# A state-space scan with an ELU layer behind it: the last scan products of one pair joined behind three units, 21 wider idle products for 30, and g's low words between y's two word sums

## The chip, the cores and the metric

The kernel runs on 1 core of one Trainium2 chip. The metric is the device time in microseconds (us). The engines are TensorE (PE; its weight loads are listed as PEld), VectorE (DVE), ScalarE (ACT), GpSimd (POOL) and SyncE (SP), which issues nearly all DMAs.

## The reference

For 4 batches x 8 heads x 768 positions, a chunked scan, then a two-layer network on the 3072 tokens:

```python
for c in range(nc):                                  # chunks of the sequence
    L = np.exp(cum[:, :, :, None] - cum[:, :, None, :]) * causal
    M = np.einsum('bhin,bhjn->bhij', Cc, Bc) * L
    y_intra = np.einsum('bhij,bhjd->bhid', M, xc)
    y_inter = np.einsum('bhin,bhnd->bhid', Cc, state) * decay_to_i[:, :, :, None]
    y[:, :, sl] = y_intra + y_inter
    state = decay_full[:, :, None, None] * state + np.sum(Bx, axis=2)
x = y.transpose(0, 2, 1, 3).reshape(B * S, H * D)    # 3072 x 256
h = x @ w_in                                         # 256 -> 2048
g = np.where(h > 0.0, h, np.exp(np.minimum(h, 0.0)) - 1.0)
out = g @ w_out                                      # 2048 -> 256
```

Inputs and output are fp32.

## The kernel before

The tokens are cut into 12 blocks of 256 (`n` = 0 to 11), worked on in pairs. The order of all instructions on each engine is written out by hand; the program runs without loops on the chip.

**Products in words.** From the pair n = 2 on, an fp32 product is made of three passes over operands that have been split into rounded words: a high word, a low word and a sum word. For y, `high_of_y` (L798, ACT) makes y1, `low_of_y` (L806, DVE) makes y0, and `both_of_y` (L816, DVE) makes the sum word y_both, one instruction for each of the two halves k of the 256 input features. For g, a *job* is a generator of three steps (`words_of_g`): ACT's high word (L922), DVE's low word (L923, tile g_low) and POOL's sum word (`sub`, L899, tile g_words). `first_of_jobs`, `second_of_jobs` and `third_of_jobs` issue these steps for jobs begun one or two rounds before.

**A stage.** For n = 4, 6, 8 the loop over `k` = 0 to 15 does three things side by side. `l1_words(n, k, m)` makes 128 rows of h for pair n (TensorE L832: passes high, low and sum; at k = 0 the sum pass is last, at other k it is first), followed on ACT and DVE by L840, L848, L860, L861 and, one round later, L867, which writes g. `l2s(count)` makes so many *units* of the second layer for the pair before (`second(n - 2)`); a unit is six products (L981), which read a job's words. `stage_scan` and the lines around it make the scan of the pair after, `m = n + 2`: `scores`, `weigh`, `sums`, `states`, and last `across` (L660, products with the state, 64 records in the trace) and `inside` (L678, products with x, 128 records). `inside` also copies the finished y to yT, half t = 0 (heads 0 to 3) with ACT (L695), half t = 1 with DVE (L693) for these stages. Both can be called for a half.

**Order around the edited places.** At `k == 13` the last scan products are issued around `l2s(3)`: for n = 4 and n = 8 all of them behind the three units, for n = 6 half t = 0 ahead of the units and half t = 1 behind them. At `k == 14` SP issues a 64-byte load (`held`, L1394) that reads yT and so waits for ACT's copies; the loads of the next stage's weight words (L765, L766) are behind it in SP's queue. At k = 14, `high_of_y` and `low_of_y` of the next pair are made, and no second or third steps of jobs. At `k == 15` (`m == MC - 1` in `l1_words`) DVE makes both halves of y_both, then g_low of one job, and POOL that job's L899; the first unit of the next stage reads it right after the first `l1_words`, whose third pass reads y_both. POOL also makes the decays of later pairs, `decay_sums` (L536), after `k == 12`.

**Start.** `small_idle_products(30, 112)` gives TensorE work on a tile of zeros while the first loads are under way: each call of matmul works on 32 rows x 64 columns of the array, at one of eight positions in turn, and is two records in the trace. The first real products are `first_low` (L501) and `first_cum` (L512, L520).

Of the kernel before, what the change touches and what calls it, by code (L numbers as in the profile page):

```python
# [13 lines left out]
F32R = mybir.dt.float32r  # L14
# [3 lines left out]
P = 128  # L18
Q = 64
BLK = 2 * P  # L20
# [13 lines left out]
def kernel(  # L34
# [36 lines left out]
    KC, MC = DM // P, DF // P  # L71
# [4 lines left out]
    ffn = ctx.enter_context(tc.tile_pool(name="ffn", bufs=2))  # L76
# [191 lines left out]
    def small_idle_products(count, cols):  # L268

        banks = [ps_idle] + [psum([P, 4, P], "ps_idle") for _ in range(3)]  # L270
        for k in range(count):
            rows, at = slice(32 * (k % 4), 32 * (k % 4) + 32), Q * (k // 4 % 2)
            nc.tensor.matmul(
                out=banks[k % 4][at:at + Q, 0:2, 0:cols], lhsT=idle[rows, 0:Q],
                rhs=idle[rows, 0:cols].unsqueeze(1).to_broadcast([32, 2, cols]),
                start=True, stop=True, tile_position=(32 * (k % 4), at), skip_group_check=True)

    small_idle_products(30, 112)
    ident = const.tile([P, P], F32, name="ident")
    make_identity(nc, ident)  # L280

# [105 lines left out]
    yT = {}  # L387
# [257 lines left out]
    def across(*ns, pool=p_a, tag="a", halves=(0, 1)):  # L645


        y = [None, None]
        for t in halves:
            y[t] = [psum([P, len(ns), 2, Q], "ps_y"), (p_a if t else pool).tile(  # L650
                [P, len(ns), 2, Q], F32, tag="a" if t else tag, name="ps_y")]
        for u in (1, 0):
            for at, n in enumerate(ns):
                for v in range(2):
                    Sx = starts.get((n, u, v))
                    if Sx is None:
                        continue
                    for q in range(2 * halves[0], 2 * halves[-1] + 2):
                        rows, col = slice(32 * q, 32 * q + 32), (64 * q + shift(n, v)) % P
                        nc.tensor.matmul(  # L660
                            out=y[q // 2][v][col:col + 64, at, u],
                            lhsT=Sx[rows].rearrange("p k d -> p (k d)"),
                            rhs=st[n]["cts"][rows, u, Q * v:Q * v + Q],
                            start=(u == 1 and at == 0), stop=False,
                            tile_position=(32 * q, col), skip_group_check=True)
        return y
# [120 lines left out]
    y_words = {}  # L787
# [20 lines left out]
                op0=ALU.mult, op1=ALU.subtract)  # L808
        y_words[n] = y1, y0

    def both_of_y(n):
        y = yT[n // 2].rearrange("p k b u i -> p k (b u i)")
        y1, y0 = y_words[n]
        both = ffn.tile([P, KC, 2 * BLK], F32R, tag="yT", name="y_both")
        for k in range(KC):
            nc.vector.scalar_tensor_tensor(  # L816
                out=both[:, k], in0=y1[:, k].bitcast(F32), scalar=1.0 - WORD,
                in1=y[:, k], op0=ALU.mult, op1=ALU.add)
        y_words[n] = y1, y0, both

    def l1_words(n, m, ahead=None, ahead_of_join=(), ahead_of_jobs=()):


        cols = slice(m % 2 * P, (m % 2 + 1) * P)
        w, w0 = k_words[m // 2]
        w1, both_w, w0 = w[:, 0, :, cols], w[:, 1, :, cols], w0[:, :, cols]
        y1, y0, both_y = y_words[n]
        high, both = psum([P, 2 * BLK], "ps_h"), psum([P, 2 * BLK], "ps_w")
        passes = [(high, w1, y1), (high, w0, y0), (both, both_w, both_y)]
        for ps, lhs, rhs in passes if n > 2 and m == 0 else passes[2:] + passes[:2]:  # L830
            for k in range(KC):
                nc.tensor.matmul(  # L832
                    out=ps, lhsT=lhs[:, k], rhs=rhs[:, k], start=k == 0 and lhs is not w0,
                    stop=k == KC - 1 and lhs is not w1)
        if ahead and m == MC - 1:
            both_of_y(ahead)
            second_of_jobs()
            third_of_jobs()
        e = ffn.tile([P, 2 * BLK], F32, tag="e", name="e", bufs=2)
        nc.scalar.activation(e, both, ACT.Copy, scale=WORD)  # L840
        first_of_jobs()
        if late:
            end_words()
        if ahead and m == MC - 2 and n > 2:
            high_of_y(ahead)
        for step in ahead_of_join:
            step()
        nc.vector.scalar_tensor_tensor(  # L848
            out=high, in0=high, scalar=WORD - 1.0, in1=e, op0=ALU.mult, op1=ALU.add)
        if ahead and m == MC - 2 and n > 2:  # L850
            low_of_y(ahead)
        for step in ahead_of_jobs:
            step()
        if not ahead or m != MC - 2:
            second_of_jobs()
        late.append((n, m, high, e))
# [106 lines left out]
    def second_of_jobs():  # L963

        while put_second:
            put_second.pop(0)()
        if len(begun_jobs) > 1:
            for j in begun_jobs[0]:
                next(j)

    def third_of_jobs():

        if len(begun_jobs) > 1:
            for j in begun_jobs.pop(0):
                next(j)
# [384 lines left out]
    for n in range(4, NP, 2):  # L1360
        m = n + 2 if n + 2 < NP else None
        steps = second(n - 2)

        def l2s(count):
            for _ in range(count):
                next(steps)

        if n == 4:
            l2s(1)
        if not m:  # L1370
            scan_pools.close()
            late_pool = ctx.enter_context(tc.tile_pool(name="late", bufs=1))
        for k in range(16):
            if k < 13 and (n > 4 or k > 4):
                to_begin.append(lambda q=k + 3: job(n - 2, q))
            elif m and k > 12:
                to_begin.append(lambda q=k - 13: job(n, q))
            if not m and k in (4, 6, 8, 10, 12, 14, 15):
                to_begin.append(lambda q=(4, 6, 8, 10, 12, 14, 15).index(k): late_job(q, late_pool))
            if k == 0 and n > 4:  # L1380
                load_words(2)
            l1_words(
                n, k, m, [lambda q=q: weigh_two(m, q) for q in (2, 3) if m and k == 10],
                [lambda: states(m + 1)] if m and k == 11 else [])
            if k != 14 or not m:
                third_of_jobs()
            if n == 4 and k < 2:
                words_of_w(k + 2)
            if n == 4 and 1 < k < 7:
                words_of_out(k + 1)  # L1390
            if k in (2, 4, 6, 8, 10) and (k > 2 or n > 4):
                load_words(k // 2 + 2)
            if m and k == 14:
                nc.sync.dma_start(out=held, in_=yT[m // 2][Q:Q + 1, 0, 0, 0, Q:Q + 16])  # L1394
            if m and k > 13:
                load_words(k - 14)
            if m:
                stage_scan(n, k)
            begin_end()
            if n == 4 and k in (1, 2):  # L1400
                low_of_w(k + 1)
                keep_words(k + 1)
            if n == 4 and 2 < k < 8:
                low_of_out(k)
            if not m:
                l2s(2)
                continue
            if k == 9:
                l2s(1)
                scores(m, m + 1, pool=p_o, tag="o")  # L1410
            l2s((2 - (n == 4 and k < 1), 2, 2, 2, 2, 2, 2, 2, 2, 1, 2, 2, 1, 0, 1, 0)[k])
            if k == 9:
                for q in range(2):
                    weigh_two(m, q)
            if k == 10:
                if m + 2 < NP:
                    for to in (m + 2, m + 3):
                        spread_cum(to)
                sums(m, m + 1, pool=p_o, tag="o")
                states(m)  # L1420
            if k == 13:
                if n == 6:
                    y = across(m, m + 1, pool=p_o, tag="o", halves=(0,))
                    inside(y, m, m + 1, t=0)
                l2s(3)
                if n == 6:
                    y = across(m, m + 1, halves=(1,))
                    inside(y, m, m + 1, t=1)
                else:
                    y = across(m, m + 1, pool=p_o, tag="o")  # L1430
                    inside(y, m, m + 1)
            if k == 12 and m + 2 < NP:
                decay_sums(m + 2)
                decay_sums(m + 3)
        if m:
            l2s(3)
        end_words()
        for _ in steps:
            pass
# [46 lines left out]
```

## Time and profile before

| | |
|---|---|
| median of 3 runs | 339.98 us (339.45 to 340.72) |
| profiled execution | 338.85 us |
| its span, first to last instruction | 337.1 us |
| mean granted TensorE clock | 0.999 |
| busy: PE, DVE, ACT, POOL | 98%, 85%, 77%, 64% of the span |
| HBM read, written | 44.53 MB, 9.63 MB |

The profile is of one execution; its times are microseconds from the first instruction. A busy TensorE is not one at its peak, since matmuls overlap. In the lists of waits, the engine and line ahead of the arrow waited for those behind it; "issue" is time in which the engine waited for nothing that the profile shows. In the timeline, the time in brackets is idle time of the engine just before, and what ended it.

### The profile page before, as it was taken

Reading aid. Unit: us, or ns where it says so; the run is one execution under the profiler, and the core shown is the slowest. Engines: PE = TensorE matmul, PEld = TensorE weight load, DVE = VectorE, ACT = ScalarE, POOL = GpSimd, SP = SyncE. Lnnn points to the kernel's source line nnn. Section 1 sums busy time; section 2 is a strip of 40 time slices with the busy share of each in tenths; the row PEclk is TensorE's granted clock in tenths of the full one; section 3 lists DMA queues with packets and bytes.
Section 4 is the critical chain, followed back from the end, with each engine's and each line's share of the span. In section 5 each row is a group of like instructions: output and inputs, shape, how many; then the busy total and the mean of one; then the engine's idle time right before and its main releaser. Section 6 shows DMA issues by size and latency. Waiting matters only on the chain.

```text
span 337.1 us, 9647 instructions
## 1 busy us (share of the span) xinstructions
PE 330.4 (98%) x3742; PEld 288.2 (85%) x3742; DVE 286.7 (85%) x511; ACT 259.0 (77%) x537; POOL 214.2 (64%) x242
## 2 busy tenths in 40 slices
PE   8899999999999999999999999999999999999995
PEld 5578888888888888888899988889889899999995
DVE  4998998889897889898989998989996978997942
ACT  5789989599857699857898866898867789897501
POOL 5454554648979396989489979388974355776000
PEclk9999999999999999999999999999999999999999
DMA  8889999553487388671769491669440762330101
GB/s 141 218 237 181 293 193 277 127 108 123 158 158 290 126 217 272 200 185 16 272 189 215 138 300 27 263 188 191 126 156 8 277 212 101 104 118 0 33 0 63
DMA packets 82956, 54.79 MB, mean 163 GB/s; under 512 B 59038, under 2 KB 68574, under 8 KB 82910
## 3 DMA queue, kind: packets, MB, share of 16 engines
q1 hardware_dynamic: 80734, 53.98, 57.4%
q8 instruction: 29, 0.48, 0.6%
q10 hardware_dynamic: 2176, 0.20, 0.5%
q14 instruction: 17, 0.14, 0.1%
HBM read 44.53 MB, written 9.63 MB: 161 GB/s over the span
## 4 chain that ended last, share of the span: by engine, by line
PE 92%; SPq 2%; DMA 2%; ACT 2%; DVE 1%; issue 0%; DVEq 0%; ACTq 0%
PE ps_o L981 24%; PE ps_h L832 20%; PE ps_o L885 12%; PE ps_h L717 11%; PE ps_w L832 10%; PE ps_both L981 6%; PE ps_y L678 3%; DMA w<-in_moe_w_in_dram 2%; PE ps_g L582 2%; PE ps_y L660 2%; PE ps_st L612 1%; PE ps_high L981 1%; SPq L156 1%; SPq L184 0%; ACT w_in L214 0%; SPq L124 0%
## 5 line engine op out<-in xcount | busy, mean ns | idle before, releaser
L899 POOL TENSOR_TENSOR g_words<-g_words,g_low 128x512 fp32r<-128x512 f32 x62 | 82.3, 1331 | 49.2 <-DVE g_low L923 25.8
L981 PE MATMUL ps_o<-o_words,g_words 128*128 128x256 f32 x448 | 83.4, 284 | 0.0
L981 PEld LDWEIGHTS ps_o<-o_words,g_words 128*128 128x128 f32 x448 | 72.9, 190 | 5.8 <-POOL g_words L899 0.8
L860 ACT ACTIVATE e<-ps_h 128x512 f32<-128x512 f32 x72 | 43.0, 597 | 35.1 <-DVE ps_h L848 35.1
L867 DVE SCALAR_TENSOR_TENSOR g<-e,ps_h 128x512 f32<-128x512 f32 x72 | 49.3, 684 | 19.0 <-ACT e L861 17.1
L981 PE MATMUL ps_o<-o_low,g_low 128*128 128x256 f32 x224 | 63.3, 283 | 0.0
L923 DVE SCALAR_TENSOR_TENSOR g_low<-g_words,g 128x512 fp32r<-128x512 f32 x72 | 63.3, 885 | 0.0
L848 DVE SCALAR_TENSOR_TENSOR ps_h<-ps_h,e 128x512 f32<-128x512 f32 x72 | 49.8, 691 | 2.7 <-ACT e L840 2.6
L832 PE MATMUL ps_w<-y_both,w_words 128*128 128x512 f32 x144 | 48.7, 419 | 0.0
L861 ACT ACTIVATE e<-e 128x512 f32<-128x512 f32 x72 | 45.5, 633 | 2.3
L717 PE MATMUL ps_h<-yT,w_in 128*128 128x256 f32 (+1 forms) x208 | 45.2, 367 | 1.6 <-ACT yT L695 1.0
L840 ACT ACTIVATE e<-ps_w 128x512 f32<-128x512 f32 x72 | 41.9, 582 | 5.4 <-PE ps_w L832 5.4
L885 PE MATMUL ps_o<-w_out,g 128*128 128x256 f32 x192 | 45.5, 380 | 0.0
L832 PE MATMUL ps_h<-y,w_words 128*128 128x512 f32 x144 | 45.3, 395 | 0.0
L832 PE MATMUL ps_h<-y,w 128*128 128x512 f32 x144 | 44.7, 391 | 0.0
L922 ACT ACTIVATE g_words<-g 128x512 fp32r<-128x512 f32 x72 | 43.6, 625 | 0.0
L981 PEld LDWEIGHTS ps_o<-o_low,g_low 128*128 128x128 f32 x224 | 42.7, 191 | 0.0
L717 PEld LDWEIGHTS ps_h<-yT,w_in 128*128 128x128 f32 x208 | 36.2, 190 | 7.5 <-POOL w_in L249 2.3
L885 PEld LDWEIGHTS ps_o<-w_out,g 128*128 128x128 f32 x192 | 36.1, 190 | 5.4
L832 PEld LDWEIGHTS ps_h<-y,w 128*128 128x128 f32 x144 | 27.0, 188 | 6.2
L832 PEld LDWEIGHTS ps_h<-y,w_words 128*128 128x128 f32 x144 | 26.6, 188 | 6.6 <-issue 0.7
L832 PEld LDWEIGHTS ps_w<-y_both,w_words 128*128 128x128 f32 x144 | 23.5, 191 | 2.0 <-ACT e L860 0.2
(132 smaller groups left out, 548.2 us busy)
## 6 DMA issues: line engine op xcount, KB each, us to landing
w_words<-w_kept SPq DMA_DIRECT2D x28, 512.0 KB
w<-w_kept SPq DMA_DIRECT2D x28, 256.0 KB
L<-flat SPq DMA_DIRECT2D x20, 256.0 KB
w<-in_moe_w_out_dram SPq DMA_DIRECT2D x8, 512.0 KB
w_kept<-w_words SPq DMA_DIRECT2D x8, 512.0 KB
w<-in_moe_w_in_dram SPq DMA_DIRECT2D x7, 512.0 KB
xr<-in_x_dram SPq DMA_DIRECT2D x24, 128.0 KB
out_dram<-eo SPq DMA_DIRECT2D x18, 128.0 KB
```

The source lines that it names most:

```text
L717: nc.tensor.matmul(out=ps[:, j, toks], lhsT=w_in[i][:, k, j * P:(j + 1) * P], rhs=yT[n // 2][:, k, n % 2].rearrange("p u i -> p (u i)")[:, ...
L832: nc.tensor.matmul(out=ps, lhsT=lhs[:, k], rhs=rhs[:, k], start=k == 0 and lhs is not w0, stop=k == KC - 1 and lhs is not w1)
L840: nc.scalar.activation(e, both, ACT.Copy, scale=WORD)
L848: nc.vector.scalar_tensor_tensor(out=high, in0=high, scalar=WORD - 1.0, in1=e, op0=ALU.mult, op1=ALU.add)
L860: nc.scalar.activation(e, high, ACT.Relu, scale=-1.0)
L861: nc.scalar.activation(e, e, ACT.Exp, scale=-1.0)
L867: nc.vector.scalar_tensor_tensor(out=g_tile(n, m // 2)[:, m % 2].rearrange("p b i -> p (b i)"), in0=e, scalar=1.0, in1=h, op0=ALU.subtract ...
L885: nc.tensor.matmul(out=o_of[n][:, ts], lhsT=g_of[n // 2, j][:, m % 2, n % 2, ts * P:(ts + 1) * P], rhs=w_out[j][:, m % 2], start=(m == 0 a ...
L899: nc.gpsimd.tensor_tensor(out=out, in0=in0, in1=in1, op=ALU.subtract)
L922: yield nc.scalar.activation(words[:, 0], g, ACT.Copy, scale=NEAR / WORD)
L923: yield nc.vector.scalar_tensor_tensor(out=low, in0=words[:, 0].bitcast(F32), scalar=WORD, in1=g, op0=ALU.mult, op1=ALU.subtract)
L981: nc.tensor.matmul(out=ps, lhsT=lhs, rhs=rhs, start=lhs is both_g and first > 0 or lhs is g1 and first > 1, stop=last and lhs is not g1, s ...
```

## The change

There are three edits.

1. `small_idle_products(21, 107)` replaces `small_idle_products(30, 112)`, and each product now writes three blocks of columns instead of two: 21 products of 321 columns for 30 of 224.
2. `both_of_y` can be called for one half k. In the last `l1_words` of a stage (for n > 2: three times in the program), the second steps of jobs (g_low) now stand between the two halves of y_both.
3. At `k == 13` of n = 6, both halves of `across` and `inside` now follow the three units in one run, as they do for n = 4 and n = 8.

```diff
-                out=banks[k % 4][at:at + Q, 0:2, 0:cols], lhsT=idle[rows, 0:Q],
-                rhs=idle[rows, 0:cols].unsqueeze(1).to_broadcast([32, 2, cols]),
+                out=banks[k % 4][at:at + Q, 0:3, 0:cols], lhsT=idle[rows, 0:Q],
+                rhs=idle[rows, 0:cols].unsqueeze(1).to_broadcast([32, 3, cols]),
...
-    small_idle_products(30, 112)
+    small_idle_products(21, 107)
...
-    def both_of_y(n):
+    def both_of_y(n, ks=range(KC)):
         y = yT[n // 2].rearrange("p k b u i -> p k (b u i)")
-        y1, y0 = y_words[n]
-        both = ffn.tile([P, KC, 2 * BLK], F32R, tag="yT", name="y_both")
-        for k in range(KC):
+        y1, y0 = y_words[n][:2]
+        if ks[0] == 0:
+            y_words[n] = y1, y0, ffn.tile([P, KC, 2 * BLK], F32R, tag="yT", name="y_both")
+        both = y_words[n][2]
+        for k in ks:
             nc.vector.scalar_tensor_tensor(
                 out=both[:, k], in0=y1[:, k].bitcast(F32), scalar=1.0 - WORD,
                 in1=y[:, k], op0=ALU.mult, op1=ALU.add)
-        y_words[n] = y1, y0, both
...
         if ahead and m == MC - 1:
-            both_of_y(ahead)
+            both_of_y(ahead, range(1) if n > 2 else range(KC))
             second_of_jobs()
+            if n > 2:
+                both_of_y(ahead, range(1, KC))
             third_of_jobs()
...
             if k == 13:
-                if n == 6:
-                    y = across(m, m + 1, pool=p_o, tag="o", halves=(0,))
-                    inside(y, m, m + 1, t=0)
                 l2s(3)
-                if n == 6:
-                    y = across(m, m + 1, halves=(1,))
-                    inside(y, m, m + 1, t=1)
-                else:
-                    y = across(m, m + 1, pool=p_o, tag="o")
-                    inside(y, m, m + 1)
+                y = across(m, m + 1, pool=p_o, tag="o")
+                inside(y, m, m + 1)
```

## The prediction

> **What bounds the kernel now.** I read the page first, then the waits of TensorE, the chain, and the timeline at the three edited places.
>
> ```profile
> PE 330.4 (98%) x3742; PEld 288.2 (85%) x3742; DVE 286.7 (85%) x511; ACT 259.0 (77%) x537; POOL 214.2 (64%) x242
> PE 92%; SPq 2%; DMA 2%; ACT 2%; DVE 1%; issue 0%; DVEq 0%; ACTq 0%
> ```
>
> TensorE is 92% of the chain that ended last, so time can only come off where TensorE stands still or works badly. The waits of its weight loads (PEld) between 130 and 337 us (total us, times, longest):
>
> ```profile
> PEld ps_o L981 <- POOL g_words L899: 0.8, 3, 0.3
> PEld ps_y L660 <- POOL g_words L899: 0.4, 1, 0.4
> PEld ps_y L678 <- issue: 0.3, 1, 0.3
> ```
>
> All of TensorE's recorded waits there come to under 3 us; the first row is one wait at each stage boundary, which the y_both edit aims at. The second is at the first half of the split scan run (n == 6).
>
> The second aim is seen in the chain (start us, us, what), around `k == 13` of n = 6, which is split, and of n = 8, which already runs as one:
>
> ```profile
> 203.13 0.92 PE ps_h L832 x4
> 204.68 0.79 PE ps_y L678 x53
> 205.47 2.33 PE ps_o L981 x18
> 208.42 0.79 PE ps_y L678 x53
> 209.87 0.93 PE ps_h L832 x4
> ...
> 253.84 0.92 PE ps_h L832 x4
> 254.76 2.15 PE ps_o L981 x18
> 256.91 0.84 PE ps_y L660 x53
> 257.75 1.44 PE ps_y L678 x90
> 259.85 0.93 PE ps_h L832 x4
> ```
>
> The same 64 + 128 records of small products (L660, L678) and 18 products of three units stand between the same two L832 groups: 209.87 - 203.13 = 6.74 us split, 259.85 - 253.84 = 6.01 us whole.
>
> **Scan run of n == 6, joined.** The saving by these rows is 6.74 - 6.01 = 0.73 us. The timeline says where: across plus inside take 1.41 us for each half (203.98 to 205.39, 207.73 to 209.14) and 2.28 us as one run (256.84 to 259.12), which is 0.54; the other 0.19 is in the two extra changes between small and large products. The other unsplit run with the same neighbours, n = 4, takes 159.00 - 152.63 = 6.37 us, since it holds a 0.34 us stall put down to issue (third row above); then the saving is 0.37. I take 0.73, because the earliest joined run (n = 2, 99.50 to 101.78) also takes 2.28 us; both ends are kept.
>
> What follows the moved products: ACT's copies of half t = 0 (L695) started early, at 207.17. They now follow the joined run, as at n = 8, where ACT's next activation (L840, 259.89) comes 0.77 us after TensorE's next L832 (259.12); now it is 0.76 (209.90 after 209.14). DVE's copies (L693) wait for products either way: 1.11 us of idle time now, 0.38 left. POOL's two L536 (4.28 us, to 209.87) hold back the L899 of job 15 to 211.12; it is first read by the second of the three units at 212.73, about 213.4, or 212.7 after the move: covered by 1.5 us. The products issue no DMA, but SP's `held` load (L1394) waits for the copies of t = 0, and the loads of the next stage's words are queued behind it. The first goes out at 208.66 and is needed by the weight load at 214.77, a lead of 6.11 us. TensorE comes 0.73 earlier and `held` 0.74 later, so about 4.64 us remain. The windows view gives 0, 135 and 377 GB/s for the three microseconds from 208.6, so the first 0.52 MB land some 3.0 us after issue, and n = 8 has no wait at a lead of 4.76. Cost taken: nothing; if that cover went, whatever the load is late.
>
> **g's low words between y's word sums.** The boundary of n = 4 in the timeline (start, us, engine, line):
>
> ```profile
> 162.06 1.28 DVE L816 SCALAR_TENSOR_TENSOR y_both<-y,yT 128x512 fp32r<-128x512 f32 x2
> 163.27 0.68 DVE L923 SCALAR_TENSOR_TENSOR g_low<-g_words,g 128x512 fp32r<-128x512 f32 x1
> 164.09 1.30 POOL L899 TENSOR_TENSOR g_words<-g_words,g_low 128x512 fp32r<-128x512 f32 x1 [3.10 <-DVE g_low L923]
> 165.44 0.30 PEld L981 LDWEIGHTS ps_o<-o_words,g_words 128*128 128x128 f32 x2 [0.30 <-POOL g_words L899]
> 294.06 1.61 POOL L899 TENSOR_TENSOR g_words<-g_words,g_low 128x512 fp32r<-128x512 f32 x1 [0.80 <-ACT e L860]
> ```
>
> The wait shows 0.30, but weight loads run ahead. From the last L832 pass to the second L981 group is 165.78 - 164.95 = 0.83 us here and 148.70 - 148.01 = 0.69 without a wait, so it costs 0.14. The other boundaries: 216.65 - 215.81 = 0.84 and 266.61 - 265.83 = 0.78, costs 0.15 and 0.09. Sum 0.38.
>
> Does the edit lift it? g_low starts one DVE slot (0.60) sooner, at 162.67, ends about 163.35, and L899 could start at 163.49 (0.14 later, as now) instead of 164.09. But y's second sum now follows on DVE from 163.27 to 163.95, and both it and L899 read two operands from SBUF. The fifth line shows that case: L923 on DVE ran from 293.84 to 294.52, L899 was issued inside it and took 1.61 us instead of 1.30, ending 1.15 us after DVE's instruction. So the words come at 163.95 + 1.15 = 165.10, not 164.79, against 165.39 now. TensorE would first load them at 165.18 without a wait: just covered. The Trainium skill, "SBUF — State Buffer", Who interferes with whom, says that a DVE instruction with two SBUF inputs and a GpSimd one that reads SBUF exclude each other, the later to issue blocking fully. By that rule the words come at 163.95 + 1.30 = 165.25, which saves 0.14 at each of the three waits but no more than 0.09 at the last: 0.37 instead of 0.38.
>
> The second y sum is read by the second matmul of TensorE's third pass, about 165.18, so 1.2 us cover it. L867 and L848 queue behind it on DVE and lose nothing: the three instructions only change places. I take 0.38; bounds 0 (the wait stays) and 0.5 (the following L923, stretched to 0.87 by L899 now, is freed as well).
>
> **Idle products.** 30 x 224 = 6720 columns become 21 x 321 = 6741, over eight array positions (four row groups, two column groups). The fullest position holds 4 x 224 = 896 columns now and 3 x 321 = 963 then. The 60 records start from 1.10 to 3.8 and the last ends at 4.38, so 7% of some 3 us is 0.2 us: L501 and L512 come up to 0.2 late. Neither a gain nor a loss is excluded, since 36 matmuls and weight loads fewer shift the place of all later ones in the instruction stream; I allow 0.2 either way. The cover: in the chain the start up to 14.9 us belongs to SP's queue and the load of w (8.31 to 14.88), ACT idles 1.39 us for w at 10.59, and DVE 0.21 at 15.64. Cost taken: nothing.
>
> Sum: 0.73 + 0.38 + 0 = 1.11 us. TensorE has no other wait behind these places, so it reaches the end whole. The profiled execution took 338.85 us (span 337.1 and 1.75 around it); it would take 337.74, with a span of 336.0. The median of the runs, 339.98, lies 1.13 above the profiled one; I take the same 1.1 off it: 338.9.
>
> **Rivals.**
> *The joined run stalls*, as at n = 4: 0.37 + 0.38 = 0.75 off, 339.2. For it: one of three joined runs stalls. Against: n = 2 and n = 8 don't. Chance 0.25.
>
> *The gains do not arrive*: the words stay late, or another engine gives the time back (DVE is at 1.00 in the windows from 210.6 on). 339.98. Against: DVE and ACT hang on TensorE's products there and move with them. Chance 0.12.
>
> *The clock stays low longer at the start: slower.* The granted clock reads 1.00 from the first window, but the same form is slower early on:
>
> ```profile
> L501 PE MATMUL ps_x<-low,ident x4: 393/421/421, 4.3 to 4.9; 128*128 128x256 bf16 x4
> ...
> L501 PE MATMUL ps_x<-low,ident x4: 272/273/273, 14.6 to 15.0; 128*128 128x256 bf16 x4
> ```
>
> The first products of L512 (from 5.28) are the last slow ones: 452 ns against a median of 268. Full speed thus comes some 4.3 us after the first idle product. If the narrower set of rounds missed that point and speed came as long again later, near 9.7, the 3.98 us of work from 5.28 to 9.26 would stretch by 0.96/0.53 (L501 to the next line, early and late), which is 3.2 us; ACT's wait of 0.87 at 14.96 absorbs part, leaving 2.3. With the gains: 339.98 + 2.3 - 1.1 = 341.2. It decides if products pause before 5.5 us. Against: 6741 columns keep the array as busy as 6720, and L501 follows without a gap. The Trainium skill, "TensorE: Matmul & The Clock Gate", section The HAM clock gate, says that the warm-up is a time of activity, not a number of matmuls; by that 21 serve as well as 30. Chance 0.05.
>
> *SP's loads land late* (lead 4.64 us against 3.0 needed): up to 0.7 back, 339.6. Chance 0.03.
>
> **Numbers.** The forecast has the remaining 0.55. A measurement of this kernel tells about 0.5%, 1.7 us, from no change; the runs shown span 1.27 us. Faster needs under 338.28: the main case lies 0.6 above that, half the runs' spread, so about a quarter of 0.55 at most; I say 0.15. Slower needs over 341.68: the clock case and a little noise, 0.06. The rest, 0.79, is the same. The range runs from the main case less 0.6 of spread and 0.3 of unknowns (338.0) to no gain plus 0.3 (340.3).
>
> **What the new profile should show.** The stretch of n == 6 near 6.0 us; L981 no longer waiting for L899 at the boundaries; there, L899 stretched to about 1.6 us; L501 starting 0 to 0.2 later; L512's second round fast. I am wrong if the joined run stays above 6.5, the boundary waits persist, or L512 and L520 run slow throughout.

## The result: slower, and the profile after

The changed kernel takes 342.67 us (median of 13 runs, 340.81 to 347.78) against 339.67 for the kernel before (13 runs beside them, 338.94 to 340.72): a ratio of 1.0072, 95% interval 1.0053 to 1.0092. (The ratios in this text leave out slow runs, here the one of 347.78 us, and are not the quotients of the medians, here 1.0088.) 338.9 was forecast, with a range up to 340.3; a slower kernel had a chance of 0.06. The profiled execution took 342.92 us, with a span of 341.2 and a mean clock of 0.995. Line numbers move: L832, L981, L899, L923, L816 and L867 of before are L833, L984, L902, L926, L818 and L870 now.

The page's busy row and its chain by engine:

```profile
PE 330.7 (97%) x3724; PEld 288.7 (85%) x3724; DVE 286.9 (84%) x511; ACT 259.7 (76%) x537; POOL 215.8 (63%) x242
PE 91%; SPq 2%; DMA 2%; ACT 2%; issue 1%; DVE 1%; DVEq 0%; ACTq 0%
```

TensorE's busy time is as before (330.7 against 330.4), while the span grew by 4.1. The one share of the chain that rose is "issue". The waits of TensorE's weight loads between 130 and 342 us (total, times, longest):

```profile
PEld ps_y L678 <- issue: 1.9, 1, 1.9
PEld ps_h L833 <- issue: 1.9, 3, 1.3
```

The row that named POOL's L902, 0.8 us in three waits, is gone, as forecast. Two rows of "issue" lead the list instead (before, the largest such row was 0.7 us, in three waits). The chain (start us, us, what) shows where. The run of n = 4 and what follows it, before:

```profile
152.63 0.92 PE ps_h L832 x4
...
157.49 0.19 issue
...
159.00 0.93 PE ps_h L832 x4
159.93 0.72 PE ps_o L981 x6
```

And after: first the joined run of n = 4, which the edit of the scan did not touch, and the stage boundary behind it; then the newly joined run of n = 6:

```profile
152.99 0.92 PE ps_h L833 x4
...
156.82 1.24 PE ps_y L678 x79
158.06 1.74 issue
159.80 0.42 PE ps_y L678 x19
...
160.87 1.25 PE ps_h L833 x4
162.13 1.28 PE ps_o L984 x6
...
167.59 0.93 PE ps_h L833 x4
...
206.95 0.92 PE ps_h L833 x4
...
212.31 0.66 PE ps_w L833 x2
212.97 0.24 PE ps_h L833
213.20 1.05 issue
...
216.29 0.92 PE ps_h L833 x4
```

The 0.19 us that the chain gave to issue in the run of n = 4 before is 1.74 now. At n = 6 the run itself takes the forecast time, 212.97 - 206.95 = 6.02 us, and then TensorE stands for 1.05 right behind it. From 160.87 on everything is slow as well: six L984 take 1.28 us, where before they took 0.72. The windows view says why (window, us, busy of PE, PEld, DVE, ACT, POOL, granted clock, DMA share, GB/s):

```profile
161.30:164.70 3.40, 3.40 (x13) 2.92 (x12) 3.19 (x6) 3.30 (x7) 0.05 (x1) 0.50 0.92 338
```

For 3.41 us, from 161.29 to 164.70, TensorE was granted half its clock. The two chains, laid beside each other, give the 4.1 us:

| stretch | before, us | after, us | difference |
|---|---|---|---|
| start to the L833 group ahead of the run of n = 4 | 152.63 | 152.99 | +0.36 (0.33 of it "issue" at 25.37, in L678) |
| run of n = 4 to the next L833 | 6.37 | 7.88 | +1.51 |
| from there over the half clock, to 167.59 | 5.19 | 6.72 | +1.53 |
| n = 6, k = 10, sums of the next pair (L612) | 3.91 | 4.45 | +0.54 (0.41 "issue" at 200.65) |
| n = 6, run and the group behind it, to 216.29 | 8.84 | 9.34 | +0.50 (0.73 saved, 1.2 lost) |
| first to second L833 group of n = 4, 6, 8 | 3.42, 3.42, 3.38 | 3.29 each | -0.35 |

### The profile page after: what moved, and what is told of

Its sections match the earlier page's. It is cut to its first block, busy times and chain, and to the rows that moved or that the text cites. A ratio compares the mean times of both kernels' runs of the same rounds, so it can differ in the third digit from the quotient of the medians.

```text
span 341.2 us, 9611 instructions
## 1 busy us (share of the span) xinstructions
PE 330.7 (97%) x3724; PEld 288.7 (85%) x3724; DVE 286.9 (84%) x511; ACT 259.7 (76%) x537; POOL 215.8 (63%) x242
## 4 chain that ended last, share of the span: by engine, by line
PE 91%; SPq 2%; DMA 2%; ACT 2%; issue 1%; DVE 1%; DVEq 0%; ACTq 0%
PE ps_o L984 24%; PE ps_h L833 20%; PE ps_o L888 12%; PE ps_h L717 11%; PE ps_w L833 10%; PE ps_both L984 6%; PE ps_y L678 3%; DMA w<-in_moe_w_in_dram 2%; PE ps_g L582 2%; PE ps_y L660 1%; PE ps_st L612 1%; PE ps_high L984 1%; SPq L156 1%; SPq L184 1%; ACT ps_mag L205 0%
## 5 line engine op out<-in xcount | busy, mean ns | idle before, releaser
L902 POOL TENSOR_TENSOR g_words<-g_words,g_low 128x512 fp32r<-128x512 f32 x62 | 83.4, 1349 | 50.9 <-ACT e L863 18.0
L984 PE MATMUL ps_o<-o_words,g_words 128*128 128x256 f32 x448 | 83.5, 284 | 0.0
L984 PEld LDWEIGHTS ps_o<-o_words,g_words 128*128 128x128 f32 x448 | 73.8, 192 | 5.3 <-issue 0.5
L870 DVE SCALAR_TENSOR_TENSOR g<-e,ps_h 128x512 f32<-128x512 f32 x72 | 49.3, 684 | 19.8 <-ACT e L864 17.7
L984 PE MATMUL ps_o<-o_low,g_low 128*128 128x256 f32 x224 | 63.6, 284 | 0.0
L926 DVE SCALAR_TENSOR_TENSOR g_low<-g_words,g 128x512 fp32r<-128x512 f32 x72 | 63.2, 883 | 0.0
L833 PE MATMUL ps_w<-y_both,w_words 128*128 128x512 f32 x144 | 49.0, 422 | 0.0
L833 PE MATMUL ps_h<-y,w_words 128*128 128x512 f32 x144 | 45.8, 398 | 1.1 <-issue 1.1
L833 PE MATMUL ps_h<-y,w 128*128 128x512 f32 x144 | 45.0, 394 | 0.0
L984 PEld LDWEIGHTS ps_o<-o_low,g_low 128*128 128x128 f32 x224 | 43.0, 192 | 0.0
L833 PEld LDWEIGHTS ps_h<-y,w 128*128 128x128 f32 x144 | 27.2, 189 | 7.5 <-issue 1.3
L833 PEld LDWEIGHTS ps_h<-y,w_words 128*128 128x128 f32 x144 | 27.0, 190 | 6.6 <-issue 0.6
L833 PEld LDWEIGHTS ps_w<-y_both,w_words 128*128 128x128 f32 x144 | 23.8, 193 | 1.9
```

What stands on the lines that cost most here:

```text
L833: nc.tensor.matmul(out=ps, lhsT=lhs[:, k], rhs=rhs[:, k], start=k == 0 and lhs is not w0, stop=k == KC - 1 and lhs is not w1)
L870: nc.vector.scalar_tensor_tensor(out=g_tile(n, m // 2)[:, m % 2].rearrange("p b i -> p (b i)"), in0=e, scalar=1.0, in1=h, op0=ALU.subtract ...
L902: nc.gpsimd.tensor_tensor(out=out, in0=in0, in1=in1, op=ALU.subtract)
L926: yield nc.vector.scalar_tensor_tensor(out=low, in0=words[:, 0].bitcast(F32), scalar=WORD, in1=g, op0=ALU.mult, op1=ALU.subtract)
L984: nc.tensor.matmul(out=ps, lhsT=lhs, rhs=rhs, start=lhs is both_g and first > 0 or lhs is g1 and first > 1, stop=last and lhs is not g1, s ...
```

## Experiments

**Theory.** TensorE stands at "issue" because its next instructions have not arrived. (A *record* is one row of the trace: a matmul or a weight load. Each small idle product makes four, two of each kind, so nine products fewer are 36 records.) The page lists their queue:

```profile
q8 instruction: 29, 0.48, 0.6%
```

29 packets of 16,384 bytes (0.48 MB in all) serve the 3,724 matmuls and 3,724 weight loads that the profile lists: 257 records for each. The Trainium skill, "Runtime: NRT & Kernel Launch", Instruction fetch mechanics, says that instructions are refilled in 16 KiB blocks of 256, and the trace agrees (257 here, and multiples of 256 between the stalls below). It also says that crossing a block's end is mostly hidden; that holds for most block ends of these traces, but not for those below.

Counting all TensorE records in order of start, with the 98 records of semaphores and drains among them, the stall at 157.84 stands at record 4032, the one at 212.81 at 5312, the one at 200.44 at 4800 and the one at 25.15 at 960: all are 192 plus a multiple of 256. The run of 64 + 128 small products is 384 records with its weight loads and takes 2.3 us (at n = 4 it has 48 + 128, 352 records), so TensorE goes through a whole block in 1.5 us. The packet ahead of the stall at n = 4 ran from 157.55 to 158.43, and TensorE resumed at 159.80; at n = 6 it ran from 211.50 to 212.84, and TensorE resumed at 214.26. A block is thus usable some 1.4 us after its packet ends. All eleven traces agree: over 309 block ends TensorE never entered a block sooner than 1.25 us after its packet's end, and every stop of more than 0.8 us between 16 us and its last product lies at a block end. (The stalls given below are gaps between the starts of two records; the chain puts 0.2 to 0.4 us less of each to issue.)

In the kernel before, the packet for the block from record 4032 began at 155.36, while the three units were still running, and only some 0.4 us were left open.

So it would be the *count* of records ahead of a run that decides whether a run stalls: let p be the number of the run's records ahead of the first block end in it. The second block end lies 256 records further on, inside the run or just behind it, and it is there that TensorE stalls. The run of n = 4 had p = 16 before, and has p = 52 with 36 records fewer at the start. **Rival 1:** the wide idle products themselves, or the start they give, do harm. **Rival 2:** the three units and the joined run are too much at n = 6 for another reason (PSUM, transfers), wherever the block ends lie. The expectations also name an *order theory*: the joined run or the order of y's sums costs the time.

**Padding the count at the start.** Nine tiny products, 36 records, behind the 21 wide ones:

```diff
+            if k == wide:
+                cols = 4
...
-    small_idle_products(21, 107)
+    small_idle_products(21, 107, 30)
```

> The changed kernel with 9 tiny idle products (12 columns each) behind the 21 wide ones: TensorE's instruction count of the kernel before (30 products) at the changed width. Fetch theory (TensorE's instructions come in packets of 16384 bytes; 36 records fewer moved the packet that was asked for at 155.36 us, among the three units of n = 4, to 157.55 us, into the run of small products, which then ran dry): the long issue stalls of the changed kernel (1.9 us at n = 4, 1.4 us at n = 6) go, the clock stays at 1.00, and the forecast gains appear: 338.6 us, 338.2 to 339.2. Width theory (the wider products or the start cost the time): as the changed kernel, 342.7 us. Order theory (the joined run or the order of y's sums costs the time): 342.7 us too.

341.16 us, ratio 1.0054 (1.0029 to 1.0078), which is neither 338.6 nor 342.7. The stall at n = 4 went, as forecast (0.27 us left). The time did not: n = 6 now stalls for 1.75 us, inside its run (at 208.95, record 5312, p = 99). The expectation had not counted on that: the same padding that saves n = 4 puts the block ends at a bad place of the joined n = 6.

**Padding it later.** The same nine tiny products, but behind the scan of n = 0, long after the start:

```diff
+    for k in range(9):
+        nc.tensor.matmul(
+            out=ps_idle[0:Q, 3, 0:4], lhsT=idle[0:32, 0:Q], rhs=idle[0:32, 0:4],
...
```

> The changed kernel with 9 tiny products added not at the start but in TensorE's idle time before the first l1 (about 11.4 us), when the clock is already at full speed. Fetch theory: what counts is the place of all later instructions in the stream, so this gives the same as the padding at the start: 338.6 us, at most 0.4 more for the 36 records themselves. Width or start theory: 342.7 us, since the start is that of the changed kernel. Order theory: 342.7 us.

341.77 us, 1.0064 (1.0040 to 1.0087): no stall at n = 4 either, and one of 2.04 us at n = 6, followed by 3.41 us at half clock from 211.77. The 338.6 expected missed for the same reason as above. For the stall at n = 4 what counts is the number of records, not the start; rival 1 loses its ground.

**Idle products alone** (edit 1 on the kernel before):

```diff
-                out=banks[k % 4][at:at + Q, 0:2, 0:cols], lhsT=idle[rows, 0:Q],
...
+                out=banks[k % 4][at:at + Q, 0:3, 0:cols], lhsT=idle[rows, 0:Q],
...
-    small_idle_products(30, 112)
+    small_idle_products(21, 107)
```

> The kernel before with the idle products alone changed (21 of 321 columns for 30 of 224). Fetch theory: the stall of about 1.9 us at n = 4 and the 3.4 us at half clock behind it appear here too; n = 6 stays split, so its 1.4 us stall does not: 342.5 us, 341.8 to 343.5, slower than before by 2 to 4. Width or start theory: the whole loss of the changed kernel without its gains, 343.8 us. Order theory: no loss, 339.7 us.

342.71 us, 1.0077 (1.0048 to 1.0107): this edit alone loses as much as the whole change. In its profile n = 4 stalls at record 4032, for 1.46 us between records, and n = 6, which is split here, does not:

```profile
158.11 1.24 issue
```

The profiled run was the fastest of the eight (340.66 us) and shows no half clock; the rest of the loss, in the slower runs, was not profiled (the mean clock of three of them was 0.995, of one 0.992).

**The other two edits, without it** (the changed kernel with 30 x 224 columns):

```diff
-                out=banks[k % 4][at:at + Q, 0:3, 0:cols], lhsT=idle[rows, 0:Q],
...
+                out=banks[k % 4][at:at + Q, 0:2, 0:cols], lhsT=idle[rows, 0:Q],
...
-    small_idle_products(21, 107)
+    small_idle_products(30, 112)
```

> The changed kernel with the 30 idle products of 224 columns back: edits 2 and 3 alone. Fetch theory: the stream lies as in the kernel before up to n = 6, and the forecast of 0.38 + 0.73 us arrives: 338.6 us, 338.2 to 339.2; only the 0.4 us stall at n = 4 stays. Width or start theory: 338.6 us too. Order theory: 342 us or more.

341.73 us, 1.0054 (1.0033 to 1.0076). The count at n = 4 is that of before, and no stall is there; the joined n = 6 has p = 99 and stalls for 1.70 us. The 338.6 expected of the fetch theory missed by 3 us, since it had counted on no block end at n = 6; the result came nearest to the order theory's 342. The next two runs take the two parts of that theory one by one.

**The joined scan run alone** (edit 3 on the kernel before):

```diff
-                if n == 6:
-                    y = across(m, m + 1, pool=p_o, tag="o", halves=(0,))
-                    inside(y, m, m + 1, t=0)
                 l2s(3)
-                if n == 6:
...
+                y = across(m, m + 1, pool=p_o, tag="o")
+                inside(y, m, m + 1)
```

> The kernel before with the scan run of n = 6 joined and nothing else. Fetch theory, sharpened by the last runs (a boundary between two packets of 256 instructions lies 99 records into the joined run and the next one 355 in; TensorE gets there about 1.5 us later, before the packet is usable): a stall of 1.5 to 2.0 us in L678 at n = 6, more than the 0.73 us that joining saves, and in some executions 3.4 us at half clock behind it: 341.5 us, 340.5 to 342.5. Order theory (it is the order of y's sums that costs): 338.9 us, the forecast gain of this edit alone.

341.09 us, 1.0037 (1.0021 to 1.0053), within the range expected of the fetch theory. Its chain in L678 at n = 6:

```profile
208.71 1.53 issue
```

The 0.73 us are saved and 1.5 put in their place. The packet ran from 207.90 to 208.82: it was asked for inside the run, and TensorE resumed at 210.23. Edit 3 loses by itself.

**The word sums alone** (edit 2 on the kernel before):

```diff
...
-            both_of_y(ahead)
+            both_of_y(ahead, range(1) if n > 2 else range(KC))
             second_of_jobs()
+            if n > 2:
+                both_of_y(ahead, range(1, KC))
```

> The kernel before with g_low between the two halves of y_both and nothing else. Fetch theory: no TensorE instruction moves, so no new stall; the waits at the three stage boundaries shrink, 0 to 0.4 us less than before: 339.3 us, 339.0 to 339.7. Order theory (this order costs the time): 341 us or more.

339.23 us against 339.62, 0.9994 (0.9977 to 1.0011): no stall, and no difference that can be told. The order of y's sums does not cost the time.

**Wide idle products kept, both runs split.** The changed kernel with the runs of n = 4 and n = 6 in halves around the units:

```diff
+                if n < 8:
+                    y = across(m, m + 1, pool=p_o, tag="o", halves=(0,))
+                    inside(y, m, m + 1, t=0)
                 l2s(3)
...
+                if n < 8:
+                    y = across(m, m + 1, halves=(1,))
+                    inside(y, m, m + 1, t=1)
...
```

> The changed kernel, its 21 wide products kept, with the scan run split around the three units at n = 6 and at n = 4 as well. Fetch theory: the three units give the packet time to arrive, so neither place stalls for more than 0.5 us and the clock stays at 1.00; each split costs its 0.4 to 0.7 us: 339.8 us, 339.2 to 340.4. Width or start theory: 342 us or more, since the start is the changed one.

340.26 us, 1.0016 (0.9995 to 1.0037). Its chain at n = 4:

```profile
153.29 0.92 PE ps_h L833 x4
...
160.04 0.93 PE ps_h L833 x4
```

6.75 us and no stall, with the 36 records still missing. With no long run at the block end, the wide products do no harm that can be told. Rival 1 falls.

**Two tiny products added to the word sums alone** (30 + 2, 8 records), to take the last 0.4 us out of n = 4:

```diff
+            if k == wide:
+                cols = 4
...
-    small_idle_products(30, 112)
+    small_idle_products(30, 112, 32)
```

> The kernel before with edit 2 and two tiny products (12 columns) behind the 30 idle ones, so that every later TensorE instruction lies 8 records later and the packet boundary in the run of n = 4 falls 8 records into it instead of 16. Fetch theory: no new stall, and the 0.4 us one at n = 4 is rarer: 339.2 us, 338.8 to 339.6; it would be faster than both kernels. If small shifts matter little: as edit 2 alone, 339.3 us. If the start matters: 0.1 to 0.2 slower than edit 2 alone.

339.48 us, 0.9993 (0.9978 to 1.0007). The 0.4 us at n = 4 is gone from its profile, but a stop of 0.87 us, which was not expected, came up at another block end (105.71, record 3008, 32 records behind the run of n = 2); the packet had begun only at 104.19. It beats neither the kernel before nor edit 2 alone by anything that can be told; inconclusive. (The tiny products of this run and the next have 8 columns in the trace, not the 12 of the expectations; the count of records is as stated.)

**Moving the block end out of n = 6.** Edits 2 and 3 with 22 tiny products (88 records), so that n = 6 gets p = 99 - 88 = 11, which should free it, while n = 2 and n = 8 get p = 80 and 94, which should make them stall:

```diff
+            if k == wide:
+                cols = 4
...
-    small_idle_products(30, 112)
+    small_idle_products(30, 112, 52)
```

> Edits 2 and 3 with the 30 idle products of before and 22 tiny ones (12 columns) behind them: every later TensorE instruction lies 88 records later. By the boundaries seen so far (records 192 + 256 j), the first boundary then falls 11 records into the joined run of n = 6 and 72 ahead of that of n = 4, both places where no run stalled by more than 0.5 us, but 80 and 94 records into the runs of n = 2 and n = 8, which never stalled before. Fetch theory: the stalls move: 1.2 to 2.0 us in L678 at n = 2 (near 102 us) and at n = 8 (near 260 us), under 0.5 us at n = 4 and n = 6, whose stretch from L832 to L832 is then 6.0 us as forecast; 342 us, 341 to 344. Rival, that the joined run of n = 6 is the slow thing by itself: the stall stays at n = 6, none at n = 2 and n = 8, 341.5 us.

346.50 us, 1.0234 (1.0188 to 1.0280), from four runs. Its chain at n = 2, n = 6 and n = 8:

```profile
102.36 3.39 issue
...
208.77 0.92 PE ps_h L835 x4
...
214.79 0.92 PE ps_h L835 x4
...
264.20 1.58 issue
```

Both stalls appeared where the count put them, in runs that nothing else had touched, and the joined n = 6 ran through in 214.79 - 208.77 = 6.02 us. Rival 2 falls: the joined run works, and is worth what was forecast, where no block end hits it. The time lies above the range expected (341 to 344); the stall at n = 2 is by far the longest (3.6 us, and then half clock from 105.68 to 109.10). Its packet began at 103.39, when TensorE had stood for 1.25 us; why so late, no run shows.

By position, over the unsplit runs of all kernels: p up to 16, or from 168 on: at most 0.4 us. p = 160: 0.87. p from 52 to 135: 1.45 to 2.04 us, and once 3.6.

The packets' starts show why both ends of the scale are harmless. With p up to 16 (eight runs) the packet began 0.3 to 1.4 us ahead of the first block end; with p from 52 to 135 (nine runs) it began 0.7 to 1.4 us behind it, once 2.7. With p from 168 on the second block end lies behind the run, among large products.

With the records of before, the runs of n = 2, 4, 6, 8, if all are joined, have p = 168, 16, 99 and 182. By these bounds no one shift of all four suits all four (p between 16 and 52 and between 135 and 160 was not met). The split at n = 6 is what keeps that packet in time: before, it ended at 207.17 and TensorE came to its block at 208.82, 1.65 us later. A shift between n = 4 and n = 6 alone was not tried. None of the kernels beats the kernel before by more than can be told.

## Why the prediction was wrong

*The step that failed* is the cost of the idle products, taken at nothing, "0.2 either way". The text named the right mechanism, "36 matmuls and weight loads fewer shift the place of all later ones in the instruction stream", in its own words for the range, and then priced it by the start, where it did not act. Measured: +3.2 us by medians for that edit alone (342.71 against 339.55 beside it). What the runs showed in its place is the stall at the block end of n = 4: 1.96 us between records in the changed kernel, with 1.5 us more for the half clock behind it.

*The second step that failed* is the joined run. Its two ends were the saving of 0.73, and 0.37 with a stall of 0.34 like that of n = 4. The one stall in view was taken for the size of such stalls. It was the tail of a longer one, most of which the packet's early start had hidden, and not a fixed cost: in the five other profiles with p = 16 at n = 4 it was 0 to 0.27 us. In the changed kernel TensorE stalled for 1.45 us between records at n = 6; with edit 3 alone, for 1.74. Nor was n = 4 a like case: its run has 16 products fewer in L660, and p = 16 where the joined run of n = 6 has 99 with edit 3 alone and 135 in the changed kernel. The rival *the joined run stalls* was right in kind; its price, 339.2, was about four times too low in the stall.

*The saving itself* was right: 6.02 us for the stretch forecast near 6.0, in the changed kernel (up to its stall) and in the padded one. It is 0.72 below the 6.74 of before.

*The low words* went as forecast in the changed kernel. At the boundary of n = 4, in the timeline after:

```profile
164.91 0.68 DVE L926 SCALAR_TENSOR_TENSOR g_low<-g_words,g 128x512 fp32r<-128x512 f32 x1
165.51 0.69 DVE L818 SCALAR_TENSOR_TENSOR y_both<-y,yT 128x512 fp32r<-128x512 f32 x1
165.73 1.62 POOL L902 TENSOR_TENSOR g_words<-g_words,g_low 128x512 fp32r<-128x512 f32 x1 [4.39 <-DVE g_low L926]
```

L902 started inside DVE's second y sum and took 1.62 us instead of 1.30, ending 1.15 after DVE's instruction, which is the row that the forecast went by; the rule of the Trainium skill cited there would have had 1.30. The boundaries gained 0.13, 0.13 and 0.09 us, 0.35 in all against 0.38. By itself the edit is too small for the medians (339.23 against 339.62, not told apart). Of the 24 boundaries in the eight profiles with this edit, 21 take 3.29 to 3.31 us between those L833 groups. The other three, all at n = 4 and with edit 2 alone among them, take 3.56 to 3.61, more than the 3.42 of before, and the loads wait for L902 there (0.43 to 0.49 us). In the changed kernel TensorE came late to n = 4, so part of that gain may be luck; what makes the difference at n = 4 was not shown.

*The clock at the start*, the rival on the slower side, was wrong in its mechanism. L501 started at 4.43 (4.32 before), within the 0 to 0.2 allowed, and its four products took 0.61 us instead of 1.03: full speed came sooner here, not later. The runs do not tie this to the width: the clock is first listed as full at 4.28 us here and 5.58 before, but over the eleven profiles at 4.20 to 7.13 with the 30 narrower products and at 4.28 to 7.18 with the 21 wide ones, so it was luck. The later half clock was a consequence of the stall, not of the idle products' width.

*SP's loads* did not show up late: behind the run of n = 6 the chain holds "issue" and TensorE's own work, and no transfer.

*The spread.* The changed kernel's runs reach from 340.81 to 347.78. Of the profiles taken, those with a half clock took 341.93, 342.92 and 345.57 us, and those with a long stall but no half clock 340.15 to 340.89. The record has the mean clock of every run, and 3.41 us at half clock take 0.005 off it: of the changed kernel's runs the six at 0.995 took 342.46 to 343.43 us, the one at 0.990 347.78, and the six at 0.999 or 1.000 340.81 to 342.87. So the spread comes in part from whether the clock drops; what makes the rest was not shown.

## What to carry to other kernels

A dense run of small products on parts of the array can use up instructions faster than they arrive, as here, at 256 in 1.5 us. Then an edit that changes the *number* of TensorE instructions far ahead, even of idle ones, can move stalls into or out of such runs: here 36 to 88 records in the first 12 us moved stalls of 1.5 to 3.6 us at 102 to 264 us. Before pricing such an edit at nothing, count the records up to each long run, see where the block ends fall in it (here 192 plus multiples of 256, read off the stalls), and read a small "issue" row as the visible end of a wait that may become whole. Large products put between the halves of a small-product run give the packet time, which at n = 6 was worth more than the 0.73 us that the split costs.

## What was not expected of the hardware

- At the stalls of n = 4 and n = 6 in six profiles the packet took 0.9 to 1.3 us, and its block could be used 1.25 to 1.42 us after the packet's end. What sets the moment of the request stays open: at n = 4 the packet began 0.3 us ahead of TensorE's passing record 3776, the block end before, in the kernel before, and 1.4 us behind it in the changed one.
- A stop of 1.96, 2.04 or 3.6 us was followed by 3.41 us at half the clock; after stops of 1.45 to 1.80 us the clock stayed at 1.00. The Trainium skill, "TensorE: Matmul & The Clock Gate", section The HAM clock gate, puts the drop behind an idle window of about 3.4 us; the half-clock time agrees with such a window (3,413 ns), but two of the three stops that led to it were shorter. In all eleven profiles any two changes of the clock lie whole multiples of 3.413 us apart (46, 60 and 29 of them from full to half), so the drop comes at a fixed tick: in the changed kernel 1.5 us after TensorE had resumed. In one stop TensorE stood for 1.92, 2.04 and 3.41 us of the 3.41 ahead of the three drops, and for at most 1.80 of any such stretch without a drop. No long stop was cut in two by a tick, so whether its length or its place decides stays open.
